# Attention mixed with a state-space branch on one core: a TensorE activity floor that runs to the last group, taps at their real weight, and the state-space output added by VectorE

## The chip, the cores and the metric

The kernel runs on one core of a Trainium2 chip. The metric is device time in microseconds (us) from one launch, lower is better. Three runs of the kernel before gave 757.92 to 760.72 us, median 759.01 us. A separate execution was recorded by the hardware profiler; it took 758.27 us, of which 756.5 us lie between its first and its last instruction (the span).

Engine names are those of the profile: PE (TensorE matmuls), PEld (its weight loads), DVE (VectorE), ACT (ScalarE), POOL (GpSimd), SP (SyncE, which here only issues DMAs).

## The reference, cut to what matters

```python
def _A_ref(x, wqkv, wo):                      # x: 1 x 2048 x 512, 32 heads of 16
    ...
    scores = jnp.einsum("bhqd,bhkd->bhqk", q, k) * scale
    p = _softmax(scores, axis=-1)
    o = jnp.einsum("bhqk,bhkd->bhqd", p, v)
    return (lambda x, *d: x.transpose(*d))(o, 0, 2, 1, 3).reshape(B, S, D) @ wo

def _B_ref(u, A_re, A_im, B_re, B_im, C_re, C_im, log_dt, Dskip):
    ...
    K = jnp.einsum("dn,dnl,dn->dl", Cc, P, dB).real       # a kernel of 2048 taps per channel
    ...                                                    # y: causal convolution of u with K, by FFT
    return y + u * Dskip[None, None, :]

g = _sigmoid((x * gate_w).sum(-1, keepdims=True))
return g * a + (1 - g) * b
```

## The kernel before

**Attention.** The scores of 32 heads are cut into 2048 tiles of 128 keys by 512 queries (`NSL`). Three tiles make a group; there are 683 groups (`NG`), counted by `g`. For each group PE multiplies keys and queries into one of two PSUM tiles (`SC0`, `SC1`; `qk`), ACT takes the exponential of the group into `ET` (or `EX`, the same ring's later slots; `ex`), and PE multiplies the result with the values into `OA` (`pv_mm`). An exponential of three tiles is 1536 columns wide ("3-wide"). In some groups the third tile is left to DVE and ACT does only two (1024 columns, "2-wide"): DVE writes scaled integers whose bits are a coarse exponential (`bits`, tile `DZ`), POOL makes three shifted copies of four such tiles (`batch`, tiles `DU`, `CUTS`), and PE multiplies all four versions with the values (`sums`). Four such tiles, from four groups, make a quad; the table `PACE` says how many quads should have begun by which group, and `WIN` how many buffers they have.

**State-space branch.** Projections and parameters come first. Then, 16 times, a block of the convolution kernel is computed by short matmuls of 48 or 64 columns, the taps, into the PSUM tile `MB` (`kstage`, `MB<-T,Z`), moved out by DVE (`Kt`, `Ks`) and written to DRAM (`gm_kd`). 32 times, the convolution itself reads it back as `H`, with the input as `U`, and multiplies the two (`ystage`, `MB<-U,H`); the results go to DRAM and come back as `Yl` and `Yl2`.

**Output.** For each of 16 blocks of 128 rows (`lt`) PE multiplies the normalized attention with `Wo` into `MB` and DVE moves the block into `fo`, which is stored (`outs`, `out_mm`). For the blocks 0 to 7 that DVE instruction also multiplies by the gate and adds `Yl`. For the blocks 8 to 15 PE adds `Yl` and `Yl2` with two matmuls by an identity (`out_y`, `idb`), and the eviction is a plain copy. Blocks 12 to 15 end after the last group, in code written out by hand (`part`, `side`, `ends`).

**The order.** Each engine's instructions are put in order when the kernel is built, by a planner (`Sched`, `Prog`) with costs written in the code; on the chip each engine runs its list in that order and waits on semaphores. For each group the planner places the exponential, the next group's `qk`, and then fills PE with other work until `OVER` us after the planned end of the exponential (`fill`). Besides, it keeps a count of TensorE activity in columns (the argument `a` of `mm`, summed in `p.act`): where a group has less than `want` (from `FILL`, `FILL2`), it adds matmuls of a zero tile `wm` (`zero`), four of 256 or 512 columns side by side into `OA`, `MB` or the next scores' bank, and one row strip beside the scores. Before, `want` is 0 from group `ZEND` on, and nothing is added there. `BG1`, `YGO` and `YLGO` name the events after which the second parameter quarter, the loads of `U` and `H`, and those of `Yl` may be issued on SP's queue; `BACK` is how far such a load may run ahead of the queue.

Of the kernel before, what the change touches and what calls it, by code (L numbers as in the profile page):

```python
# [11 lines left out]
ALU = mybir.AluOpType  # L12
# [3 lines left out]
D = 512  # L16
# [15 lines left out]
VLD = .0545  # L32
LAZY = 9
PDEL = 0.3
ZEND = 200
OUTP = 6
YSEG = 4
KSEG = 4
FILL = 1500
FILL2 = 1500  # L40
OVER = 0.4
REST = (14, 0, 1792, 425)
DLAG = .6
PLAG = .4
# [13 lines left out]
CUTS = (26, 56, 94)  # L58
XB = 128 * (127 - math.log2(5.3794))
WIN = ((0, 560, 2, 4), (560, 679, 4, 6))  # L60
PACE = ((0, 0), (40, 0), (90, 0), (140, 0), (200, 12.6), (270, 18.2), (340, 35.7), (420, 54.1), (500, 70.9), (570, 87.7), (630, 102.7), (683, 115.95))
DVEND = 679
YLP = 4.5
YQ = 0
XGO = 'g14'
YGO = 'g130'
YLGO = 'K14'
BG0 = 'g0'
BG1 = 'K1'
BG2 = 'K4'  # L70
BG3 = 'g0'
TP = 2
# [6 lines left out]
NZ = 2  # L79
US = [2, 12, 3]  # L80
HS = [4, 48, 8]
BACK = 0.3
UN4 = 4
HN = 1
UB = 1.10
# [643 lines left out]
def record(nc, p, B, ins):  # L729
# [709 lines left out]
    def kstage(blk):  # L1439
# [8 lines left out]
        for k in range(8):  # L1448
            for t in range(4):
                if t % KSEG == 0:  # L1450
                    yield ("PE", .062 * KSEG + (.06 if k + t == 0 else 0))
                lo, n = (0, 64) if t % 2 == 0 else (16, 48)
                at = (t // 2 * 112 + t % 2 * 64) * CB
                for j in range(4):
                    x = k ^ j
                    ch = 32 * (blk % 4) + 4 * (j // 2) + 2 * (j % 2) + 8 * (x % 4) + x // 4
                    mm(lambda j=j, x=x, lo=lo, n=n: MB(64 * x + lo, [[1, n]], 32 * j, 32), lambda ch=ch, t=t: Z(t // 2 * 4096 + ch, [[128, 32]]),
                       lambda ch=ch, at=at, n=n: Tm(at + 2 * (ch % 32), [[2 * CB, n // 2], [1, 2]]),
                       zk + [(Tm, (t, m), blk) for m in range(3 if t % 2 else 4)], ky, k + t == 0, t == 3, pos=(0, 32 * j),
                       c=.062 if j == 0 else 0, a=n // 2, cfg="C")  # L1460
# [202 lines left out]
    def outs():  # L1663
# [16 lines left out]
        for lt in range(13):  # L1680
            if lt == 12:
                yield ("AFTER", "n29")
            yield ("LOCK", "MB")
            for pi in range(4 if lt < 12 else 3):
                yield ("PE", MM)
                out_mm(lt, (MB, 0, 0), pi)
            for k in range(2 if lt >= 8 else 0):
                yield ("PE", MM)
                out_y(lt, (MB, 0, 0), k)
            if lt == 12:  # L1690
                break
            yield ("DVE", .7, -1)
            o, off, W = fo, (lt % 4) * D, [(fo, lt % 4, lt)]
            if lt < 8:
                op("DVE", lambda v, lt=lt, o=o, off=off: v.scalar_tensor_tensor(o(off, [[1, D]]), MB(0, [[1, D]]), B["g"](lt, [[1, 1]]),
                                                                                Yl(8 * lt, [[128, D // 8], [1, 8]]), ALU.mult, ALU.add),
                   [(MB, 0, ('o', lt))] + [(Yl, k) for k in range(NBLK)] + key("g"), W, c=.7)
            else:
                op("DVE", lambda v, o=o, off=off: v.tensor_copy(o(off, [[1, D]]), MB(0, [[1, D]])), [(MB, 0, ('o', lt))], W, c=.62)
# [145 lines left out]
    for g in range(NG):  # L1845
# [25 lines left out]
                    sch.force(f"dvp{i}")  # L1871
                sch.add(bits(g + 1), 0)
        t = p.tm["ACT"]
        want = (FILL if g < REST[3] else FILL2) * (t - t0) / 1.335 + min(max(lack, -256), 768)
        t0 = t
        sch.rest = g < REST[3] and g % REST[0] < REST[1]
        if sch.rest:
            want = max(want, REST[2])
        sch.fill(t, t + OVER, want if g < ZEND else 0)
        lack = want - p.act if g < ZEND else 0  # L1880
        p.act = bare = 0
        while lack >= 256 and p.tm["PE"] < t + OVER and g < NG - 1:
            z = zbank()
# [7 lines left out]
        p.act = 0  # L1891
    o = SC[(NG - 2) % 2]
    banks = [(MB, 0, 0), (o, 0, 0), (o, 512, 1), (o, 1024, 2)]
    part = [(lt, k) for lt in (13, 14) for k in range(5)]

    def piece(lt, k):
        if k < 3:
# [33 lines left out]
        side(0, h)  # L1931
    for i in range(3):
        out_mm(12 + i, banks[i], 3, True)
    for k in (1, 2, 3, 4, 5):
        for h in range(2):
            side(k, h)
    tail = [(fo, i * D, [(fo, i, 12 + i)]) for i in range(4)] + [(Qm, 0, [(Qm, (0, j), 'o') for j in range(4)])]
    ends = ((0, "DVE", 0, D), (1, "ACT", 0, D), (2, "DVE", 0, D), (3, "ACT", 0, w), (3, "DVE", w, w))
    for (i, eng, at, n), (f, o, W) in zip(ends, tail):
        b, off, sl = sides[1] if at else banks[i]  # L1940
        R = [(b, sl, ('o', 12 + i) if n == D else ('o', 15, at // w))]
        if eng == "DVE":
            op("DVE", lambda v, f=f, o=o, b=b, off=off, n=n: v.tensor_copy(f(o, [[1, n]]), b(off, [[1, n]])), R, W, c=.07 + n * .00108)
# [39 lines left out]
```

## Time and profile before

| | |
|---|---|
| median of 3 runs | 759.01 us (757.92 to 760.72) |
| profiled execution | 758.27 us |
| its span, first to last instruction | 756.5 us |
| mean granted TensorE clock | 0.986 of full speed |
| ACT busy | 737.4 us, 97% of the span |
| PE busy | 685.9 us, 91% |
| DVE busy | 656.2 us, 87% |
| POOL busy | 359.4 us, 48% |
| exponentials on ACT | 683, of them 453 2-wide and 230 3-wide |
| tiles left to DVE | 452, which is 113 quads |

The profile shows one execution. A group of instructions there has a line of the kernel, an engine, an operation and its tiles (`ET<-SC` is read "from `SC` into `ET`"), a count, the engine's busy time in it, and the idle time just before it with what ended that wait. A row of the timeline has a start, a length and the instructions merged in it.

### The profile page before, as it was taken

What the parts mean: (1) busy time and instruction counts of PE and PEld (TensorE: products, weight loads), DVE (VectorE), ACT (ScalarE), POOL (GpSimd) and SP (SyncE); (2) the same over time, 40 slices, a digit from 0 to 9 for tenths busy, and PEclk for the clock granted to TensorE, in tenths of its full rate; (3) what the DMA queues carried; (4) which work ended last, traced back from release to release, by engine and by line L of the source; (5) the groups of instructions that cost most, each with busy time, mean ns of one, the idle gap of its engine ahead of it and who ended that gap; (6) DMA issues with size and microseconds to landing.
All of it is one profiled execution on the core that took longest, in us unless ns stands there. A gap on an engine that the chain in (4) does not pass through costs nothing.

```text
span 756.5 us, 31064 instructions
## 1 busy us (share of the span) xinstructions
PE 685.9 (91%) x13740; PEld 288.5 (38%) x13741; DVE 656.2 (87%) x1096; ACT 737.4 (97%) x695; POOL 359.4 (48%) x356
## 2 busy tenths in 40 slices
PE   7777878887899987898999999999999999999998
PEld 3222333432445343355344444443453443222222
DVE  8999998689998898899898989898887878687886
ACT  7999999999999999999999999999999999999996
POOL 5000000000066631222777776767758777677683
PEclk9999999999999998999999999999999999999999
DMA  9657710421825777654478686613766784200001
GB/s 216 163 150 141 114 43 9 107 58 50 222 55 130 194 201 187 188 121 102 134 191 227 172 209 153 189 22 75 207 150 161 171 221 87 36 26 26 26 15 37
DMA packets 176587, 94.32 MB, mean 125 GB/s; under 512 B 116802, under 2 KB 159940, under 8 KB 176452
## 3 DMA queue, kind: packets, MB, share of 16 engines
q1 hardware_dynamic: 175636, 91.61, 49.5%
q8 instruction: 108, 1.77, 1.0%
q10 hardware_dynamic: 816, 0.72, 0.3%
q14 instruction: 27, 0.22, 0.1%
HBM read 63.42 MB, written 18.90 MB: 109 GB/s over the span
## 4 chain that ended last, share of the span: by engine, by line
ACT 76%; PE 18%; DVE 4%; POOL 1%; issue 1%; DVEq 0%; POOLq 0%
ACT ET L1007 68%; ACT EX L1007 8%; PE SC L744 7%; PE OA L744 7%; PE MB L744 3%; DVE DZ L1029 2%; POOL DU L1048 1%; DVE T L1093 1%; DVE OT L1069 0%; DVE ON L1084 0%; DVE ft L1093 0%; DVE Ks L1471 0%; DVE Qm L1819 0%; DVE OnT L1089 0%; DVE Kt L1468 0%
## 5 line engine op out<-in xcount | busy, mean ns | idle before, releaser
L1007 ACT ACTIVATE ET<-SC 128x1024 bf16<-128x1024 f32 (+1 forms) x618 | 675.0, 1341 | 8.2 <-PE SC L744 6.7
L1048 POOL INT64_ADD DU<-DZ x336 | 348.2, 1051 | 324.4 <-DVE T L1093 191.8
L1029 DVE TENSOR_SCALAR DZ<-SC 128x512 uint16<-128x512 f32 x452 | 302.3, 684 | 67.4 <-PE SC L744 55.0
L744 PE MATMUL SC<-Qm,KT 32*128 32x512 bf16 x2048 | 277.4, 389 | 60.1 <-ACT ET L1007 54.0
L744 PEld LDWEIGHTS SC<-Qm,KT 32*128 32x128 bf16 x2048 | 70.7, 91 | 265.5 <-ACT ET L1007 194.3
L744 PE MATMUL OA<-ET,VE 128*32 128x512 bf16 x1461 | 148.0, 393 | 1.2 <-DVE VE L853 0.9
L744 PE MATMUL OA<-DU,VE 128*32 128x512 bf16 x1356 | 130.1, 386 | 2.1 <-POOL DU L1048 2.0
L744 PEld LDWEIGHTS MB<-U,H 128*32 128x32 bf16 x4096 | 85.5, 144 | 29.4 <-issue 20.3
L744 PE MATMUL MB<-U,H 128*32 128x128 bf16 (+7 forms) x4096 | 94.6, 227 | 0.0
L1007 ACT ACTIVATE EX<-SC 128x1024 bf16<-128x1024 f32 (+1 forms) x65 | 69.0, 1273 | 0.0
L744 PEld LDWEIGHTS OA<-ET,VE 128*32 128x32 bf16 x1461 | 37.6, 96 | 59.7 <-issue 54.1
L1093 DVE TENSOR_TENSOR T<-B,DT 128x1536 bf16<-128x1536 bf16 x64 | 59.7, 966 | 0.0
L744 PEld LDWEIGHTS OA<-DU,VE 128*32 128x32 bf16 x1356 | 36.0, 98 | 41.2 <-issue 26.0
L744 PE MATMUL OA<-wm 128*32 128x256 bf16 (+3 forms) x242 | 47.6, 350 | 1.2 <-DVE idf L799 1.2
L744 PEld LDWEIGHTS MB<-T,Z 128*32 128x32 bf16 x2048 | 43.1, 156 | 11.6 <-issue 7.9
L744 PE MATMUL MB<-T,Z 128*32 128x48 bf16 (+1 forms) x2048 | 46.2, 236 | 0.1
L744 PE MATMUL OA<-DZ,VE 128*32 128x512 bf16 x452 | 45.0, 388 | 0.0
L1093 DVE TENSOR_TENSOR ft<-Z 128x512 f32<-128x512 f32 (+3 forms) x48 | 40.2, 862 | 0.1
L1093 DVE TENSOR_TENSOR Z<-ft,ft 128x1024 bf16<-128x1024 bf16 (+3 forms) x56 | 31.7, 566 | 0.4
L1621 POOL MEMSET gt<- 128x128 f32 x1 | 0.2, 206 | 58.1 <-DVE pt L1093 58.1
L1574 DVE TENSOR_TENSOR Yst<-MB,gt 128x512 bf16<-128x512 f32 x32 | 21.8, 681 | 6.7 <-PE MB L744 6.6
L1069 DVE STREAM_TRANSPOSE OT<-OA 128x512 f32<-128x512 f32 x32 | 22.6, 707 | 1.8 <-PE OA L744 1.6
(139 smaller groups left out, 428.9 us busy)
## 6 DMA issues: line engine op xcount, KB each, us to landing
H<-gm_kd SPq DMA_DIRECT2D x128, 256.0 KB, 4.0
U<-gm_xs SPq DMA_DIRECT2D x128, 134.2 KB, 3.4
T<-B SPq DMA_DIRECT2D x16, 256.0 KB, 3.6
gm_yd<-Yst SPq DMA_DIRECT2D x64, 64.0 KB, 3.1
gm_kd<-Ks SPq DMA_DIRECT2D x64, 40.0 KB, 2.2
gm_xs<-xP SPq DMA_DIRECT2D x16, 136.0 KB, 5.2
gm_pd<-L SPq DMA_DIRECT2D x8, 256.0 KB, 4.2
Z<-gm_pd SPq DMA_DIRECT2D x8, 256.0 KB, 3.5
```

The costliest lines, as they stand in the source:

```text
L744: op("PE", lambda t: t.matmul(out(), lhsT(), rhs(), start=start, stop=stop, skip_group_check=True, **kw), R, W, c=c, lat=.15, a=a, cfg=cfg)
L1007: op("ACT", lambda a: a.activation(E(at, [[1, 512 * n]]), sc(0, [[1, 512 * n]]), AF.Exp, scale=DH ** -0.5), [(sc, i, g) for i in range(n)] ...
L1029: op("DVE", lambda v: v.tensor_scalar(z.u16(512 * k, [[1, 512]]), sc(1024, [[1, 512]]), XS, XB, ALU.mult, ALU.add), [(sc, 2, g)], [(z, k, ...
L1048: op("POOL", lambda v, u=u, cut=cut: v.int64_add(u.u64(), z.u64(), cut * 0x0001000100010001), R, [(u, 0, i)], c=1.016, lat=.09, lk=True)
L1069: op("DVE", lambda v: v.transpose(OT(512 * w, [[1, 512]]), OA(0, [[1, 512]])), [(OA, 0, b)], [(OT, w, b)], c=.64)
L1093: op(eng, lambda v: v.tensor_tensor(o(), a(), b_(), f), R, W, c=c)
L1574: op("DVE", lambda v, w=w, h=h: v.tensor_tensor(Yst(1024 * w + 4 * h, [[128, R8], [8, 16], [1, 4]]), MB(0, [[1, R8], [R8, 16], [NC, 4]]), ...
L1621: op("POOL", lambda v: v.memset(B["gt"](0, [[1, NC]]), 0.0), [], [(B["gt"], j) for j in range(8)], c=.3)
```

## The change

The activity floor now goes on to the last group: up to group `ZEND` (200 before, 260 now) with 1500 columns for every 1.335 us of planned exponential, and after it with `LOW`, 1300; a group's surplus is carried over up to 256 columns in both stretches (`SURP`). The taps of `kstage` count a quarter of their columns as activity, where they counted half. PE may be filled to 0.5 us past the exponential, not 0.4. `PACE` asks for more quads early and in all (last entry 118.95, before 115.95). The events behind which loads are issued, and `BACK`, are changed. For output blocks 8 to 11, 12, 14 and the second half of 15, the matmul that adds `Yl` is left out and the DVE eviction adds it; blocks 13 and the first half of 15 keep it, since ACT evicts them. `Yl2` stays on PE.

```diff
-ZEND = 200
+ZEND = 260
...
+LOW = 1300
+SURP = 256
 FILL2 = 1500
-OVER = 0.4
+OVER = 0.5
...
-PACE = ((0, 0), (40, 0), (90, 0), (140, 0), (200, 12.6), (270, 18.2), (340, 35.7), (420, 54.1), (500, 70.9), (570, 87.7), (630, 102.7), (683, 115.95))
+PACE = ((0, 0), (40, 0), (90, 0), (140, 0), (200, 15.0), (270, 28.3), (340, 39.5), (420, 53.9), (500, 73.9), (570, 90.7), (630, 105.7), (683, 118.95))
...
-YGO = 'g130'
-YLGO = 'K14'
+YGO = 'projs'
+YLGO = 'K15'
 BG0 = 'g0'
-BG1 = 'K1'
+BG1 = 'g0'
...
-BACK = 0.3
+BACK = 0.4
...
-                       c=.062 if j == 0 else 0, a=n // 2, cfg="C")
+                       c=.062 if j == 0 else 0, a=n // 4, cfg="C")
...
-            for k in range(2 if lt >= 8 else 0):
+            if lt >= 8:
                 yield ("PE", MM)
-                out_y(lt, (MB, 0, 0), k)
+                out_y(lt, (MB, 0, 0), 1)
...
-                op("DVE", lambda v, o=o, off=off: v.tensor_copy(o(off, [[1, D]]), MB(0, [[1, D]])), [(MB, 0, ('o', lt))], W, c=.62)
+                op("DVE", lambda v, lt=lt, o=o, off=off: v.tensor_tensor(o(off, [[1, D]]), MB(0, [[1, D]]), Yl(8 * lt, [[128, D // 8], [1, 8]]), ALU.add),
+                   [(MB, 0, ('o', lt))] + [(Yl, k) for k in range(NBLK)], W, c=.68)
...
-        want = (FILL if g < REST[3] else FILL2) * (t - t0) / 1.335 + min(max(lack, -256), 768)
+        want = (FILL if g < ZEND else LOW) * (t - t0) / 1.335 + min(max(lack, -256 if g < ZEND else -SURP), 768)
...
-        sch.fill(t, t + OVER, want if g < ZEND else 0)
-        lack = want - p.act if g < ZEND else 0
+        sch.fill(t, t + OVER, want)
+        lack = want - p.act
...
-    part = [(lt, k) for lt in (13, 14) for k in range(5)]
+    part = [(13, k) for k in range(5)] + [(14, k) for k in (0, 1, 2, 4)]
...
-    for k in (1, 2, 3, 4, 5):
-        for h in range(2):
-            side(k, h)
+    for k, h in ((1, 0), (1, 1), (2, 0), (2, 1), (3, 0), (4, 0), (4, 1), (5, 0), (5, 1)):
+        side(k, h)
```

Since the planner decides, the whole order moves. Three places show it.

On ACT, each row is a run of exponentials of one width. Before, groups 206 to 243:

```order
L1007 ACTIVATE ET<-SC 128x1024 x4
L1007 ACTIVATE ET<-SC 128x1536 x8
L1007 ACTIVATE ET<-SC 128x1024 x4
L1007 ACTIVATE ET<-SC 128x1536 x12
L1007 ACTIVATE ET<-SC 128x1024 x4
L1007 ACTIVATE ET<-SC 128x1536 x6
```

Now, groups 190 to 241:

```order
L1009 ACTIVATE ET<-SC 128x1536 x2
L1009 ACTIVATE ET<-SC 128x1024 x20
L1009 ACTIVATE ET<-SC 128x1536
L1009 ACTIVATE ET<-SC 128x1024 x20
L1009 ACTIVATE ET<-SC 128x1536
L1009 ACTIVATE ET<-SC 128x1024 x8
```

Groups 200 to 259 had 24 2-wide exponentials and have 52; groups 280 to 399 had 113 and have 81; over the whole kernel 453 became 461 and 230 3-wide ones became 222. The quads rise from 113 to 115.

On PE, groups 577 to 582, behind the last convolution step and ahead of the first output block (`OA` sums values, `DU`, `DZ`, `ET` and `EX` are the exponentials' tiles). Before:

```order
L744 MATMUL OA<-DU_68,VE 32x512 x4
L744 MATMUL OA<-ET,VE 32x512 x4
L744 MATMUL SC<-Qm,KT 128x512 x6
L744 MATMUL OA<-EX,VE 32x512 x4
L744 MATMUL SC<-Qm,KT 128x512 x6
L744 MATMUL OA<-DZ_65,VE 32x512 x4
L744 MATMUL OA<-EX,VE 32x512 x2
L744 MATMUL OA<-ET,VE 32x512 x2
L744 MATMUL SC<-Qm,KT 128x512 x3
L744 MATMUL OA<-DU_69,VE 32x512 x4
```

Groups 575 to 577 now:

```order
L746 MATMUL OA<-DZ_64,VE 32x512 x4
L746 MATMUL MB<-Wo,OnR_73 32x512 x4
L746 MATMUL OA<-DU_66,VE 32x512 x4
L746 MATMUL SC<-Qm,KT 128x512 x3
L746 MATMUL OA<-EX,VE 32x512 x4
L746 MATMUL OA<-DU_67,VE 32x512 x4
L746 MATMUL MB<-Wo,OnR_73 32x512 x8
L746 MATMUL SC<-Qm,KT 128x512 x3
```

The output blocks (`MB<-Wo,OnR`) began in groups 580 to 599 and now begin in groups 560 to 579, so that this stretch has them between the scores.

At the end of PE's list, the last output blocks. Before:

```order
L744 MATMUL SC<-Wo,OnT_72 128x512 x2
L744 MATMUL SC<-Wo,OnT_72 128x256 x4
L744 MATMUL SC<-Yl,idb 128x256 x2
L744 MATMUL SC<-Yl_103,idb 128x256 x2
L744 MATMUL SC<-Wo,OnT_72 128x256 x2
```

Now:

```order
L746 MATMUL SC<-Wo,OnT_72 128x512 x2
L746 MATMUL SC<-Wo,OnT_72 128x256 x4
L746 MATMUL SC<-Yl,idb 128x256
L746 MATMUL SC<-Yl_103,idb 128x256 x2
L746 MATMUL SC<-Wo,OnT_72 128x256 x2
```

One half-width matmul fewer stands ahead of the last one. The zero matmuls go from 259 to 374: by groups, from 127 to 126 in 0 to 79, from 103 to 136 in 80 to 139, from 29 to 100 in 140 to 259, and from 0 to 12 from there on. On SP's queue the four loads of the second parameter quarter (`Z_154`) move from behind the first block written to `gm_kd` to ahead of it, and the first load of `U` comes 15 rows of that queue later.

More of the change, by code (lines that the diff above doesn't have):

```diff
@@ L1942, in record @@
         if eng == "DVE":
-            op("DVE", lambda v, f=f, o=o, b=b, off=off, n=n: v.tensor_copy(f(o, [[1, n]]), b(off, [[1, n]])), R, W, c=.07 + n * .00108)
+            op("DVE", lambda v, f=f, o=o, b=b, off=off, n=n, at=at, i=i: v.tensor_tensor(f(o, [[1, n]]), b(off, [[1, n]]), Yl(8 * (12 + i) + 16 * at, [[128, n // 8], [1, 8]]), ALU.add),
+               R + [(Yl, x) for x in range(NBLK)], W, c=.07 + n * .0012)
         else:
```

## Prediction

> **What bounds the kernel now.** First the page: how long each engine works, and the groups of ACT and DVE.
>
> ```profile
> span 756.5 us, 31064 instructions
> PE 685.9 (91%) x13740; PEld 288.5 (38%) x13741; DVE 656.2 (87%) x1096; ACT 737.4 (97%) x695; POOL 359.4 (48%) x356
> L1007 ACT ACTIVATE ET<-SC 128x1024 bf16<-128x1024 f32 (+1 forms) x618 | 675.0, 1341 | 8.2 <-PE SC L744 6.7
> L1029 DVE TENSOR_SCALAR DZ<-SC 128x512 uint16<-128x512 f32 x452 | 302.3, 684 | 67.4 <-PE SC L744 55.0
> ```
>
> ACT is busy for 97% of the span, and nearly all of it is the exponentials, with only 8.2 us of idle time before them, 6.7 of it ended by PE's scores. So the time falls in only two ways: ACT gets less to do, or it waits less. An engine beside it counts only where it makes ACT wait. The chain of waits gives the price of an exponential, since it shows runs without a gap:
>
> ```profile
> 13.63 57.76 ACT ET L1007 x43
> 646.09 2.75 ACT EX L1007 x3
> ```
>
> The first run is 3-wide: 57.76 / 43 = 1.343 us each. The second is 2-wide: 2.75 / 3 = 0.917. A tile given to DVE takes 0.426 us from ACT.
>
> Next, where ACT waits. The timeline of ACT shows these idle times (in brackets) in three neighbourhoods:
>
> ```profile
> 283.50 1.02 ACT L1007 ACTIVATE ET<-SC 128x1024 bf16<-128x1024 f32 x1 [0.21 <-PE SC L744]
> 285.00 18.06 ACT L1007 ACTIVATE ET<-SC 128x1024 bf16<-128x1024 f32 x14 [0.47 <-PE SC L744]
> 303.53 1.02 ACT L1007 ACTIVATE ET<-SC 128x1024 bf16<-128x1024 f32 x1 [0.47 <-PE SC L744]
> 304.89 40.95 ACT L1007 ACTIVATE ET<-SC 128x1024 bf16<-128x1024 f32 x34 [0.34 <-PE SC L744]
> 346.10 58.02 ACT L1007 ACTIVATE ET<-SC 128x1024 bf16<-128x1024 f32 x59 [0.25 <-PE SC L744]
> 651.80 2.12 ACT L1007 ACTIVATE ET<-SC 128x1024 bf16<-128x1024 f32 x2 [0.21 <-PE SC L744]
> ```
>
> One exponential alone lasts 1.02 us, but in a run only 0.917 pass from one to the next. So whenever ACT stops, 0.10 us is lost besides the idle time shown. What is special about these moments is in the windows, whose column after POOL is the granted TensorE clock:
>
> ```profile
> 277.90:281.30 3.40, 1.83 (x50) 0.83 (x46) 3.40 (x6) 3.40 (x3) 0.00 (x0) 1.00 0.54 135
> 281.40:284.80 3.40, 3.40 (x56) 1.28 (x52) 2.70 (x5) 2.92 (x3) 0.00 (x0) 0.50 0.88 247
> 295.00:298.40 3.40, 2.10 (x69) 1.14 (x59) 2.76 (x6) 3.40 (x4) 0.00 (x0) 1.00 0.81 245
> 298.50:305.30 6.80, 6.21 (x127) 2.88 (x124) 5.69 (x10) 5.99 (x6) 0.00 (x0) 0.50 0.77 215
> 339.40:342.80 3.40, 1.66 (x37) 0.67 (x25) 3.40 (x7) 3.40 (x4) 0.00 (x0) 1.00 0.52 129
> 342.80:346.20 3.40, 3.40 (x95) 1.80 (x98) 2.44 (x6) 3.15 (x4) 0.00 (x0) 0.50 0.90 259
> 646.60:650.00 3.40, 2.16 (x24) 0.52 (x22) 3.21 (x6) 3.40 (x5) 0.73 (x1) 1.00 0.39 82
> 650.00:653.40 3.40, 3.40 (x29) 0.61 (x26) 1.91 (x4) 3.12 (x4) 2.33 (x3) 0.50 0.02 5
> 73.20:76.60 3.40, 3.40 (x31) 0.73 (x29) 2.26 (x4) 3.24 (x3) 0.00 (x0) 0.50 0.29 52
> 140.00:160.00 20.00, 16.96 (x484) 9.52 (x475) 14.17 (x34) 20.00 (x16) 0.00 (x0) 1.00 0.39 104
> ```
>
> In the first eight rows the clock falls to half four times, for 3.4 or 6.8 us, and ACT is short of work in or right behind it. Ahead of each fall PE (first number after the length) was busy for 1.66 to 2.16 of 3.40 us, 49 to 64%. From 140 to 160 us, where the kernel adds zero matmuls, it is busy for 85% and the clock stays full.
>
> The Trainium skill ("TensorE: Matmul & The Clock Gate", Part 1 on the HAM clock gate) says the clock goes to half after about one idle window of 3.4 us, and that gaps over about 3 us are to be avoided. By that rule a PE half busy would keep its clock, and a floor of activity would buy nothing. The lengths of 3.4 and 6.8 us agree with the window; the falls at 49 to 64% busy do not agree with a need for idleness, and I go by the rows.
>
> ACT's remaining waits lie mostly in one stretch of dense 2-wide groups with taps and convolution (its row from 400 to 560 us):
>
> ```profile
> L1007 ACT ACTIVATE ET<-SC 128x1024 bf16<-128x1024 f32 (+1 forms) x157 | 151.5, 1092 | 4.5 <-PE SC L744 3.4
> ```
>
> **The change part by part.**
>
> *Quads.* 230 3-wide exponentials become 222, so 8 x 0.426 = **3.4 us** less on ACT. It costs DVE 8 x 0.684 = 5.5 us and, with three shifted versions of each tile, PE 24 more value matmuls, six quartets. A quartet takes PE 0.22 us, the step between these starts:
>
> ```profile
> 287.76 0.40 PE L744 MATMUL OA<-DU,VE 128*32 128x512 bf16 x4
> 287.99 0.39 PE L744 MATMUL OA<-ET,VE 128*32 128x512 bf16 x4
> 130.92 0.38 PE L744 MATMUL SC<-Qm,KT 32*128 32x512 bf16 x1 [0.41 <-ACT ET L1007]
> 130.92 0.39 PE L744 MATMUL OA<-wm 32*128 32x512 bf16 x1
> ```
>
> That is 1.3 us on PE. DVE has 5.8 us free from 140 to 160 alone, and the second parameter quarter, whose loads now come earlier on SP's queue, can fill that. If the cover is gone, a late DVE holds the scores' bank and ACT waits for up to those 5.5 us.
>
> *Zero matmuls.* Of the 115 added, 23 are row strips beside the scores, which start with them (130.92 both) and cost nothing. The other 92 are 23 quartets, 15 of 256 columns at half of 0.22 (an estimate from the full one) and 8 of 512: 15 x 0.11 + 8 x 0.22 = 3.4 us of PE, most of it in groups 80 to 259, where PE had 15% free at 140 to 160. I take 0 on the path; uncovered it is 3.4.
>
> *The clock.* The falls at 281, 298 and 343 us stand in groups 216 to 270, from which the floor was missing and which were 3-wide. Now those groups are nearly all 2-wide with three shifted versions each. Counting the order by the 0.22 quartet, groups 220 to 239 had 18 value quartets in 6 x 0.917 + 14 x 1.343 = 24.3 us and have 31 in 18.8 us; per us, 0.74 became 1.65, and 56 of 80 short convolution steps remain. The fall at 650 stands between the last convolution step and the first output block (groups 577 to 582, shown with the change); output quartets now stand there. So I expect these four gone. The rows give 0.21 + 0.47 + 0.47 + 0.34 + 0.25 + 0.21 = 1.95 us of idle time, and six stops at 0.10: **2.6 us**. Bounds: 0 if the clock falls elsewhere instead, and 2.6 if it doesn't. PE's order up to group 79 changes in one place only, so the fall at 73 us (the row ahead of the last) stays.
>
> *Fill to 0.5 us.* PE's work beside the scores may start the next scores 0.1 us later. The waits of PE's weight loads say how often that can matter:
>
> ```profile
> PEld SC L744 <- ACT ET L1007: 197.3, 397, 1.4
> PEld SC L744 <- ACT EX L1007: 22.7, 48, 0.8
> ```
>
> In 445 of 683 groups PE stood waiting for ACT, and 0.1 us is hidden. In the other 238 it might not be: 0 to 23.8 us. ACT's 6.7 us of waits for scores came in 20 pieces; so I stay near zero and take 0, keeping the other end as a rival.
>
> *Dense groups moved early.* Groups 200 to 259 get 28 more 2-wide exponentials, groups 280 to 399 have 32 fewer. The stretch from 400 to 560 lost 4.5 us in 160, 0.5 per 18 us; three more such stretches early cost 1.5, and six lighter ones later return up to that. I take 0, bounds +2.5 and -4.5 (all of those waits gone).
>
> *Evictions.* Five quartets of `Yl` leave `MB`: 1.1 us of PE, mostly in the last 100 us, off the path.
>
> ```profile
> L1574 DVE TENSOR_TENSOR Yst<-MB,gt 128x512 bf16<-128x512 f32 x32 | 21.8, 681 | 6.7 <-PE MB L744 6.6
> L1695 DVE SCALAR_TENSOR_TENSOR fo<-MB,g,Yl 128x512 bf16<-128x512 f32 x8 | 5.9, 743 | 0.3 <-PE MB L744 0.3
> L1699 DVE CAST fo<-MB 128x512 bf16<-128x512 f32 x4 | 2.7, 680 | 0.0
> ```
>
> The add of PSUM and `Yl` is not in the trace; it lies between 0.680 (copy) and 0.743 (multiply and add `Yl`). The two-operand instruction nearest to it takes 0.681. At the very end, PE:
>
> ```profile
> 752.35 0.60 PE L744 MATMUL SC<-Yl,idb 128*128 128x256 bf16 x4
> 752.78 0.38 PE L744 MATMUL SC<-Wo,OnT 128*128 128x256 bf16 x2
> 753.20 0.42 DVE L1943 CAST Qm<-SC 128x256 bf16<-128x256 f32 x1 [0.17 <-PE SC L744]
> 753.81 0.45 SPq L1947 DMA_DIRECT2D out_dram<-Qm x1
> ```
>
> Four `Yl` matmuls take 0.43 us, one goes: **0.1 us** from the last chain, 0 if the adding eviction is slower by 0.06. The full-width one that goes from block 14 stood under the last DVE transposes and brings nothing.
>
> *Loads.* `U` and `H` are asked for later by 15 rows of SP's queue, behind the parameters. No wait of PE for a load of `U` or `H` is among the longest waits of the trace. I take 0; one `H` load that is issued late costs at most its way of 4.0 us:
>
> ```profile
> H<-gm_kd SPq DMA_DIRECT2D x128, 256.0 KB, 4.0
> ```
>
> **Sum**: 3.4 + 2.6 + 0.1 = 6.1 us. The profiled execution took 758.27, so it would take 752.2; it lay 0.7 below the median of the three runs, 759.01, and against that the forecast is **752.9 us**.
>
> **The rivals.**
>
> 1. *The floor doesn't do what it says*: the clock falls as often, in other groups (280 to 340, now lighter). Only quads and tail remain: 759.0 - 3.5 = 755.5. For it: the floor is counted by the planner's clock, not the chip's, and places only 12 of its zeros past group 259. Against: those groups have more value work than the ones that fell. The skill's rule above gives the same 755.5, since the falls would not be PE's half-idleness.
> 2. *Waits come back in the dense early groups*, 2.5 us: 755.4. Together with 1: 758.0. For it: ACT waits there already in the row from 400 to 560.
> 3. *Waits shrink*, since groups 280 to 399 are lighter: up to 4.5 less, 748.4.
> 4. *Slower*: the fill to 0.5 us. The place is the scores of the 238 groups in which PE was not waiting. If half of them pass on the full 0.1 us, it is +11.9: 759.0 - 6.1 + 11.9 = 764.8. It makes the kernel slower by over 0.5% from 99 groups on (6.1 + 3.8 = 9.9 us). Against: ACT stopped for scores only 20 times.
>
> **How the numbers follow.** Forecast (750.5 to 755.2): 0.52. Rival 1: 0.14. Rival 2: 0.10. Both: 0.07. Rival 3: 0.10. Rival 4: 0.07. The range from 748.5 to 757.5 holds all but rivals 4, both, and some of 3: about 0.8. A measurement of this kernel can tell about 0.5% from no change, which is 755.2 to 762.8. Below it are the forecast, rival 3 and somewhat less than half of rivals 1 and 2, which stand at its edge: 0.72. Within it: the rest of these and both together, 0.21. Above: 0.07.
>
> **What would show it.** Right: no row of half clock between 200 and 740 us; 461 2-wide exponentials; ACT's idle time before exponentials at about 6 us instead of 8.2; three `Yl` matmuls of 256 columns at the end. Wrong: rows of half clock in new places (rival 1); new stops of ACT at full clock between 220 and 290 us (rival 2) or many of about 0.1 us everywhere, with fewer waits of PE's weight loads for ACT than 445 (rival 4).

## The result and the profile after

The changed kernel takes **754.44 us** (753.50 to 756.03, 6 runs); the kernel before, measured beside it, took 758.46 (757.62 to 760.72, 6 runs). The ratio is 0.9944, with a 95% interval of 0.9924 to 0.9963: 4.2 us less, within 2.8 to 5.8. The profiled execution took 754.11 (span 752.3); that of before took 758.27 (756.5).

The page of the changed kernel, with its engines and the groups of ACT and DVE:

```profile
span 752.3 us, 31289 instructions
PE 686.2 (91%) x13857; PEld 288.5 (38%) x13858; DVE 659.4 (88%) x1104; ACT 732.2 (97%) x695; POOL 365.1 (49%) x362
L1009 ACT ACTIVATE ET<-SC 128x1024 bf16<-128x1024 f32 (+1 forms) x619 | 671.6, 1336 | 8.9 <-PE SC L746 5.1
L1031 DVE TENSOR_SCALAR DZ<-SC 128x512 uint16<-128x512 f32 x460 | 307.8, 684 | 64.8 <-PE SC L746 53.2
```

There are eight DVE tiles more (460 against 452, which is 115 quads against 113; where an expectation below writes 114 and 106 quads, it means these two numbers), and ACT is busy for 5.2 us less. But its idle time ahead of the exponentials has not fallen from 8.2 to 6, as the prediction wanted; it is 8.9.

The clock, by windows (the column after POOL is the granted TensorE clock), first for before and then for the change:

```profile
200.00:740.00 540.00, 512.62 (x10338) 217.99 (x10330) 465.83 (x754) 532.48 (x535) 343.58 (x332) 0.98 0.52 132
```

```profile
200.00:740.00 540.00, 516.30 (x10367) 217.44 (x10363) 463.81 (x751) 532.69 (x541) 353.40 (x342) 1.00 0.54 133
```

The falls between 200 and 740 us are gone. Yet ACT is busy for as long in these 540 us (532.69 against 532.48): nothing was won there in waits. The timeline of ACT shows what came in their place:

```profile
217.74 1.94 ACT L1009 ACTIVATE ET<-SC 128x1024 bf16<-128x1024 f32 x2 [0.36 <-PE OA L746]
220.03 19.80 ACT L1009 ACTIVATE ET<-SC 128x1024 bf16<-128x1024 f32 x21 [0.35 <-PE SC L746]
240.28 3.77 ACT L1009 ACTIVATE ET<-SC 128x1024 bf16<-128x1024 f32 x4 [0.45 <-PE SC L746]
244.68 14.94 ACT L1009 ACTIVATE ET<-SC 128x1024 bf16<-128x1024 f32 x15 [0.64 <-PE SC L746]
260.11 21.14 ACT L1009 ACTIVATE ET<-SC 128x1024 bf16<-128x1024 f32 x22 [0.49 <-PE OA L746]
287.94 12.45 ACT L1009 ACTIVATE ET<-SC 128x1024 bf16<-128x1024 f32 x13 [0.64 <-PE SC L746]
432.77 1.02 ACT L1009 ACTIVATE ET<-SC 128x1024 bf16<-128x1024 f32 x1 [0.83 <-PE SC L746]
434.38 4.69 ACT L1009 ACTIVATE ET<-SC 128x1024 bf16<-128x1024 f32 x5 [0.58 <-PE SC L746]
```

All of these stops are at full clock, and six of the eight stand in the dense early groups, at 217 to 288 us.

To add them up, each exponential is held against its pitch (0.917 us 2-wide, 1.343 3-wide): what it ends later behind its predecessor is ACT's waiting. In us, by stretches of groups:

| groups | before | after |
|---|---|---|
| 0–139 | 0.97 | 2.29 |
| 140–259 | 3.35 (2.29 of it at falls) | 4.79 |
| 260–399 | 3.57 (0.37 at a fall) | 3.73 |
| 400–499 | 4.10 | 1.87 |
| 500–682 | 1.55 (0.76 at a fall) | 0.15 |
| all | 13.5 | 12.8 |

The span fell by 4.2 us: 3.4 by the quads, 0.7 by waits. The falls took 3.4 us with them, but waits at full clock and a window of half clock at 14.7 us gave most of it back.

What ends the stop at 244.68 is seen on four engines. Beside ACT's row above, the rows are those of DVE, POOL and PE from the changed kernel's timeline:

```profile
241.51 1.22 DVE L1095 TENSOR_TENSOR ft<-Z 128x1024 f32<-128x1024 f32 x1
242.83 3.07 POOL L1050 INT64_ADD DU<-DZ  x3 [1.46 <-DVE ft L1095]
243.92 0.40 PE L746 MATMUL OA<-DU,VE 128*32 128x512 bf16 x4 [0.59 <-POOL DU L1050]
244.25 0.40 PE L746 MATMUL SC<-Qm,KT 32*128 32x512 bf16 x4
```

POOL waits 1.46 us until DVE's two-operand instruction is done, so its shifted version comes late; PE waits 0.59 us for that version, and the next scores stand behind it in PE's order. ACT then waits 0.64 us for the scores. The stop at 287.94 has the same form; of the other four early stops none has a wait of PE for `DU` ahead of it.

At 432 us it is a load. SP's queue and PE:

```profile
426.55 0.52 SPq L1532 DMA_DIRECT2D U<-gm_xs  x1
427.12 2.52 SPq L1544 DMA_DIRECT2D H<-gm_kd  x4
431.23 1.18 PE L746 MATMUL MB<-U,H 128*32 128x128 bf16 x48 [0.77 <-DMA H<-gm_kd]
433.57 0.45 PE L746 MATMUL MB<-U,H 128*32 128x128 bf16 x16 [0.47 <-DMA H<-gm_kd]
```

SP issues without a pause, so the four `H` loads go out from 427.12 on, and PE gets to their matmuls before the last ones land. ACT loses 2.2 us in groups 363 to 369.

The end of the program:

```profile
748.01 0.49 PE L746 MATMUL SC<-Yl,idb 128*128 128x256 bf16 x3
748.13 1.31 SPq L1950 DMA_DIRECT2D out_dram<-fo  x3
748.76 0.42 DVE L1945 TENSOR_TENSOR Qm<-SC,Yl 128x256 bf16<-128x256 f32 x1
749.49 0.45 SPq L1950 DMA_DIRECT2D out_dram<-Qm  x1
```

There are three `Yl` matmuls of 256 columns, as predicted, and the last eviction ends at 749.18. But SP is busy with three other stores until 749.44, and the last store begins right behind them, so the tenth of a microsecond is not won.

### The profile page after: what moved, and what is told of

Its sections match the earlier page's. It is cut to its first block, busy times and chain, and to the rows that moved or that the text cites. A ratio compares the mean times of both kernels' runs of the same rounds, so it can differ in the third digit from the quotient of the medians.

```text
span 752.3 us, 31289 instructions
## 1 busy us (share of the span) xinstructions
PE 686.2 (91%) x13857; PEld 288.5 (38%) x13858; DVE 659.4 (88%) x1104; ACT 732.2 (97%) x695; POOL 365.1 (49%) x362
## 3 DMA queue, kind: packets, MB, share of 16 engines
q8 instruction: 109, 1.79, 1.0%
## 4 chain that ended last, share of the span: by engine, by line
ACT 77%; PE 17%; DVE 3%; DMA 1%; POOL 1%; issue 0%; SPq 0%; DVEq 0%; ACTq 0%; POOLq 0%
ACT ET L1009 70%; PE SC L746 7%; ACT EX L1009 7%; PE OA L746 7%; PE MB L746 4%; DMA H<-gm_kd 1%; DVE DZ L1031 1%; POOL DU L1050 1%; DVE ft L1095 0%; DVE Qm L862 0%; DVE T L1095 0%; DVE Qm L1822 0%; DVE OT L1071 0%; DVE OnT L1091 0%; DVE KT L846 0%
## 5 line engine op out<-in xcount | busy, mean ns | idle before, releaser
L1050 POOL INT64_ADD DU<-DZ x342 | 353.9, 1049 | 372.7 <-DVE DZ L1031 257.3
L1031 DVE TENSOR_SCALAR DZ<-SC 128x512 uint16<-128x512 f32 x460 | 307.8, 684 | 64.8 <-PE SC L746 53.2
L746 PE MATMUL SC<-Qm,KT 32*128 32x512 bf16 x2048 | 274.6, 385 | 50.9 <-ACT ET L1009 44.9
L746 PE MATMUL OA<-DU,VE 128*32 128x512 bf16 x1380 | 132.4, 385 | 2.5 <-POOL DU L1050 2.4
L746 PEld LDWEIGHTS MB<-U,H 128*32 128x32 bf16 x4096 | 83.5, 144 | 30.7 <-issue 20.5
L746 PE MATMUL MB<-U,H 128*32 128x128 bf16 (+7 forms) x4096 | 92.6, 226 | 2.1 <-DMA H<-gm_kd 1.5
L746 PE MATMUL OA<-wm 128*32 128x256 bf16 (+3 forms) x317 | 59.9, 343 | 1.2 <-DVE idf L801 1.2
L746 PE MATMUL MB<-T,Z 128*32 128x64 bf16 (+1 forms) x2048 | 46.6, 235 | 0.0
L1095 DVE TENSOR_TENSOR ft<-Z,DM 128x1024 bf16<-128x1024 bf16 x32 | 21.4, 680 | 0.0
```

The lines of the kernel that those rows point to most:

```text
L746: op("PE", lambda t: t.matmul(out(), lhsT(), rhs(), start=start, stop=stop, skip_group_check=True, **kw), R, W, c=c, lat=.15, a=a, cfg=cfg)
L1031: op("DVE", lambda v: v.tensor_scalar(z.u16(512 * k, [[1, 512]]), sc(1024, [[1, 512]]), XS, XB, ALU.mult, ALU.add), [(sc, 2, g)], [(z, k, ...
L1050: op("POOL", lambda v, u=u, cut=cut: v.int64_add(u.u64(), z.u64(), cut * 0x0001000100010001), R, [(u, 0, i)], c=1.016, lat=.09, lk=True)
L1095: op(eng, lambda v: v.tensor_tensor(o(), a(), b_(), f), R, W, c=c)
```

## The experiments

The two theories at the start: **A**, the time comes from the quads and from the falls that are gone, and the floor's zeros hold the clock; **B**, the new stops in dense groups (by zeros, quads or their packing) eat what the falls gave. Every run here was compared with the kernel before on its own chip; ratios are to that.

**The order without its zeros.** Zero matmuls from group 140 on are planned, but not emitted.

```
        zero(...)
+       if p.q >= 140: p.drop.add(len(p.log) - 1)
```

> The changed kernel's order, with the 111 zero matmuls that it adds from group 140 on left out of the program and nothing else moved. Theory A (the added zeros hold the clock): half-clock windows return between 200 and 450 us, three or more, and the time is 1 to 3 us above the changed kernel, about 756 us. Rival B (the quads' value matmuls, moved early, hold the clock, and the zeros only stand in the way): no half-clock window between 200 and 740 us, and the stops of ACT between 215 and 290 us, which lose 4.8 us there now, shrink; the time is 1 to 3 us below the changed kernel, 751.5 to 753.5 us.

756.63 us, ratio 0.9967 (0.9949 to 0.9985). That is above the change by 2.2 us in the medians and by 1.7 in the ratios, whose intervals overlap a little. The stops stay, though two of them are shorter (at groups 156 and 198, 0.30 and 0.32 us lost instead of 0.46 and 0.60). ACT's timeline of this kernel:

```profile
264.27 3.82 ACT L1012 ACTIVATE ET<-SC 128x1024 bf16<-128x1024 f32 x4 [0.50 <-PE SC L747]
268.52 20.41 ACT L1012 ACTIVATE ET<-SC 128x1024 bf16<-128x1024 f32 x21 [0.42 <-PE SC L747]
289.56 2.85 ACT L1012 ACTIVATE ET<-SC 128x1024 bf16<-128x1024 f32 x3 [0.64 <-PE SC L747]
```

The first of these rows stands right behind a fall of the clock at 261 us, the only one of this profile between 200 and 740 us, where theory A wanted three or more. By the mean granted clocks of the runs, 3.7 windows of half clock (3.41 us each) passed per run; of the changed kernel, 1.8; of before, 6.5. So the zeros do hold the clock, and for the most part they are not what makes the dense stops. But of the 4.6 windows that the change saves, 2.8 are saved without these zeros, by the denser order and the zeros ahead of group 140.

**The old pace of quads in the changed kernel** (113 quads, floor and all else kept): `PACE` as before.

> The changed kernel with the old table of quads (453 2-wide exponentials, 113 quads, few of them in groups 200 to 279), the floor, the taps' weight, the 0.5 us and the evictions kept; the planner then adds 419 zeros. Theory A (quads are worth 3.4 us, and what the dense early groups lose in waits comes from elsewhere): 3.4 us above the changed kernel, 757.9 us. Rival B (the dense early groups give 3.4 us and take about as much in new waits): within 1 us of the changed kernel, 753.5 to 755.5 us, with no half-clock window after 100 us and fewer stops between 200 and 290 us.

759.66 us, ratio 1.0005 (0.9989 to 1.0021), 5.2 above the change and 1.8 above theory A's time, although only 2.2 windows of half clock passed per run. With the floor and without the two added quads, the change is worth nothing.

**The floor in the old kernel, at the falls only**: zeros are allowed in groups 212–220, 229–241, 263–270 and 574–583, and the rest is planned anew behind them.

```
+LOWS = ((212, 221), (229, 242), (263, 271), (574, 584))
+        on = g < ZEND or any(a <= g < b for a, b in LOWS)
-        lack = want - p.act if g < ZEND else 0
+        lack = want - p.act if on else 0
```

> The kernel before with zeros allowed in four short runs of groups (212 to 220, 229 to 241, 263 to 270, 574 to 583), 52 zero matmuls more, the same 453 2-wide exponentials in the same groups. Theory A (a fall of the clock costs about 0.8 us in stops of ACT, four of them 3.4 us): the four falls go and the time is 3 to 3.4 us below the kernel before, 755.1 to 755.5 us. Rival B (zeros and a new order bring waits of the same size): the falls go, and the time stays within 1 us of the kernel before.

758.72 us, ratio 0.9994 (0.9981 to 1.0007). No half clock from 18 to 755 us in the profile, 2.5 windows per run, and no gain, as rival B had it. The planner placed later work otherwise, and new waits of 1.7 us came in groups 300 to 319.

**The fill to 0.5 us in the old kernel**: `OVER = 0.5`.

> The kernel before with PE filled to 0.5 us past the exponential, not 0.4, alone. Theory A (scores that start up to 0.4 us late cost nothing, and few are later): within 1 us of the kernel before, 757.5 to 759.5 us. Rival B (late scores pass the 0.1 us on to ACT): 2 us or more above the kernel before, 760.5 us or more, with more than 20 stops of ACT for the scores.

763.00 us, ratio 1.0048 (1.0030 to 1.0067). The time is rival B's, but not its cause: ACT's waits are 14.2 us, against 13.5 before, and PE ended 18 of its stops ahead of exponentials, where rival B wanted more than 20. The loss is at the end, in PE's rows:

```profile
750.29 0.43 PE L744 MATMUL MB<-Yl,idb 128*32 128x512 bf16 x4
751.67 1.05 PE L744 MATMUL MB<-Wo,OnR 128*32 128x512 bf16 x16 [0.95 <-DVE fo L1699]
752.53 0.66 PE L744 MATMUL MB<-Yl,idb 128*32 128x512 bf16 x8
754.06 0.83 PE L744 MATMUL MB<-Wo,OnT 128*32 128x512 bf16 x12 [0.86 <-DVE fo L1699]
```

Output blocks that had stood between scores were pushed past the last exponential, where one waits for the other's eviction. ACT's wait for its first eviction grew from 3.69 to 8.41 us.

**Zeros put into the old order.** Nothing is planned anew: a quartet of 512-column zeros behind the fill of the same groups where a sum in `OA` is open (32 quartets).

```
+        for k, q, b in reversed(prog.inj):
+            log[k:k] = [(prog.op, q, a) for a in zeros(wm, bufs["OA"], b)]
```

> The kernel before, order word for word as it was, with 32 quartets of 512-column zero matmuls put in behind the fill of groups 212-220, 229-241, 263-270 and 574-583 (nothing else moved, nothing left out). They add to the open sum in OA. Theory A (the falls at 281, 298, 343 and 650 us cost what the profile's pitch shows, 3.4 us, and zeros beside ACT cost nothing): no half clock between 200 and 700 us in the profile, median 758.7 - 3.4 = 755.3, ratio 0.9955 (about 0.994 to 0.997). Rival B (a fall only uncovers a wait that comes anyway, a few groups later; this is why the replanned order with zeros gained nothing): the falls go and the time stays, 758 to 759, ratio 0.999 or more. Rival C (the zeros themselves make scores late): new stops of ACT at the inserted places, time up by up to 32 x 0.22 = 7 us.

758.44 us, ratio 0.9990 (0.9972 to 1.0008). By the mean clocks 2.4 windows of half clock passed per run instead of 6.5, and the time hardly moved. But two of the falls stayed in the profile, at 283 and 297 us, where too few sums were open, so this run alone does not settle the price of a fall. It showed another wait, on PE inside a run of equal matmuls:

```profile
426.02 0.82 PE L757 MATMUL OA<-DU,VE 128*32 128x512 bf16 x10 [0.56 <-issue]
```

**`BACK` at 0.3 in the changed kernel**; the order is the same up to group 340.

> The changed kernel with BACK back at 0.3: the order is the same up to about group 340, and the state-space loads and matmuls from there to group 500 are planned earlier or later by some groups. Theory A (the stop of PE at 431-434 us for an H load, 2.2 us of ACT, comes from the loads being issued late by the new BACK and SP's queue): that stop goes, ACT's excess in groups 340 to 479 falls from about 5.5 to 3.5, median about 752.3, ratio to before 0.992. Rival B (the wait moves to another H load or to other groups): 754.4 within 0.8, ratio 0.994.

753.34 us, ratio 0.9929 (0.9906 to 0.9953), the lowest of all, though its interval overlaps the change's. The stop at 432 us is gone (2.17 us in groups 360 to 379 became 0.39), so it was the place of that load. But the waits came back behind it: groups 380 to 399 waited 1.79 us instead of 0.75, and groups 400 to 499 2.74 instead of 1.87, so that groups 360 to 499 waited 4.9 in all, against 4.8. This is rival B for the waits. The first of the new ones is ended by this stop of PE:

```profile
450.92 0.76 PE L746 MATMUL MB<-U,H 128*32 128x128 bf16 x36
452.67 0.62 PE L746 MATMUL MB<-U,H 128*32 128x120 bf16 x28 [0.99 <-issue]
```

**All quads and the floor, but a later pace.**

```
-PACE = (..., (200, 15.0), (270, 28.3), (340, 39.5), (420, 53.9), ...
+PACE = (..., (200, 12.6), (270, 20.2), (340, 37.1), (420, 54.1), ...
```

> The changed kernel with all its 114 quads and its floor, but a pace near the old one for groups 160 to 420 (12.6, 20.2, 37.1, 54.1 quads at 200, 270, 340, 420): groups 200 to 279 have 39 2-wide exponentials instead of 67, groups 280 to 399 have 112 instead of 81. Theory A (the 3.6 us of new waits in groups 140 to 259 come from the dense early packing): ACT's excess in groups 140 to 259 falls from 4.8 to about 1.5, groups 280 to 399 gain back less than 1.5; the clock stays full by the floor; median 754.4 - 2 = 752.4, ratio 0.992. Rival B (stops go with 2-wide groups wherever they stand): what is saved early is lost in 280 to 399, 754.4 within 0.8. Rival C (the floor does not hold in 3-wide groups, which fell before): half clock at 260 to 345 us again, 756 to 758.

755.62 us, ratio 0.9958 (0.9943 to 0.9972). Groups 140 to 259 waited 2.8 instead of 4.8 us, and 260 to 399 waited 5.7 instead of 3.7: of the three, rival B is nearest, and 2.0 us of stops went with the 2-wide groups. The rest did not. In ACT's rows of this kernel, the first two stops of the change stand where they stood, and a long one is new:

```profile
217.73 1.94 ACT L1009 ACTIVATE ET<-SC 128x1024 bf16<-128x1024 f32 x2 [0.37 <-PE OA L746]
220.02 42.52 ACT L1009 ACTIVATE ET<-SC 128x1024 bf16<-128x1024 f32 x43 [0.35 <-PE SC L746]
263.47 3.84 ACT L1009 ACTIVATE ET<-SC 128x1024 bf16<-128x1024 f32 x4 [0.93 <-PE SC L746]
267.88 33.08 ACT L1009 ACTIVATE ET<-SC 128x1024 bf16<-128x1024 f32 x28 [0.57 <-PE SC L746]
```

Held against the old pace (ratio 1.0005), the same kernel with two quads, eight tiles, fewer, it prices the quads in their place: 0.0047 of 759 is 3.6 us, with about 1.6 either way by the two intervals, near the 3.4 that was worked out. The order moved between the two as well, so the nearness is in part luck.

**The evictions undone in the changed kernel**, for blocks 8 to 12 (block 12 then holds its `Yl` part twice).

```
+            for k in range(2 if lt >= 8 else 0): ... out_y(lt, (MB, 0, 0), k)
-                op("DVE", ... v.tensor_tensor(..., MB(0, [[1, D]]), Yl(...), ALU.add) ...)
+                op("DVE", ... v.tensor_copy(..., MB(0, [[1, D]])) ...)
```

> The changed kernel with the eviction edits of output blocks 1 to 11 undone (both Yl quartets in MB for blocks 8 to 11, plain copies for 1 to 7 as before for their second half; the tail edits stay). Theory A (those quartets lie beside ACT's work and cost nothing): 754.4 within 0.6, ratio 0.9945. Rival B (as with the fill of 0.5 alone, four more quartets push the last output blocks behind the last exponential): later part and tail longer by 1 us or more, 755.4 or above, ratio 0.996 or more, and the last group of exponentials to the end of the span longer than 10.6 us.

755.43 us, ratio 0.9945 (0.9924 to 0.9966): no difference, since the kernel before took 759.15 on that chip. Five dense stops of the change came back at the same groups with the same lengths (0.47, 0.45, 0.56, 0.74 and 0.75 us lost at groups 156, 158, 179, 183 and 226): they belong to the order, not to chance.

**Zeros beside the values, old order kept**: 32 quartets in groups 213 to 271 and 12 in 573 to 581, each right behind a value quartet.

> The kernel before with its order kept and zero quartets of 512 columns put right behind value quartets: 32 in groups 213-271 (256 PE instructions, as many as one 16 KB fetch of them, so that the fetches stand where they stood from group 272 on) and 12 in groups 573-581. Nothing is left out. The earlier insertion left two of the falls (windows at 0.316 and 0.337 of full-array columns) and moved PE's fetches by 192 instructions from group 271 to 574. Theory A (the falls cost 3.4 to 4 us and zeros beside values cost little): no half clock from 200 to 740 us, no new stop of PE inside a run of equal matmuls, median about 755.5, ratio 0.9955 or less. Rival B (what the falls give back is lost again, as in the two kernels with zeros before): ratio 0.998 or more although the falls are gone.

758.24 us, ratio 1.0000 (0.9984 to 1.0016). The clock is full; one stretch by windows, of before and then of this kernel:

```profile
277.90:305.30 27.40, 21.80 (x492) 10.29 (x488) 23.75 (x38) 25.91 (x22) 3.67 (x3) 0.81 0.71 190
```

```profile
277.90:305.30 27.40, 24.16 (x618) 11.70 (x610) 24.30 (x40) 27.28 (x23) 4.48 (x4) 1.00 0.77 205
```

ACT is busy for 27.28 us of it, against 25.91, and groups 140 to 259 wait 2.16 instead of 3.35 us. So the falls there do cost time, but of the 2.3 us that the pitch puts down to them, 1.2 came back. The zeros, or the waits that the falls had hidden, cost something too; at the fourth place:

```profile
647.28 2.11 ACT L1030 ACTIVATE EX<-SC 128x1024 bf16<-128x1024 f32 x2 [0.92 <-PE SC L767]
```

Groups 560 to 579 wait 1.42 us that they did not wait before, twice what the fall at 650 had cost. In all, ACT waits 0.9 us less than before where 3.4 us of falls went, and the ratio shows none of it: rival B.

**The quads alone in the old kernel** (only `PACE`, as in the later pace, so 115 quads).

> The kernel before with 114 quads instead of 106 and nothing else (pace 12.6, 20.2, 37.1, 54.1 at 200, 270, 340, 420, then that of the changed kernel; 461 2-wide exponentials). Theory A (a quad is worth 0.426 us of ACT, DVE and PE cover it): median 759.1 - 3.4 = 755.7, ratio 0.9955, with falls of the clock as before. Rival B (DVE at 87% cannot cover them, new waits for scores behind DVE's reads of the bank): 757.5 or more, ratio 0.998 or more, DVE's TENSOR_SCALAR ending ACT's new stops.

762.89 us, ratio 1.0054 (1.0032 to 1.0075), slower. The time is rival B's, but not its cause: PE waited 0.9 us for DVE's reads of the scores' bank, as before. ACT's waits are 22.8 us. Some are falls in dense groups; others are POOL again, with DVE's `T` ahead of it:

```profile
508.40:511.80 3.40, 3.40 (x41) 0.91 (x36) 3.19 (x7) 2.79 (x3) 2.15 (x3) 0.50 0.02 5
505.40 3.10 POOL L1048 INT64_ADD DU<-DZ  x3 [1.03 <-DVE T L1093]
506.49 0.40 PE L744 MATMUL OA<-DU,VE 128*32 128x512 bf16 x4 [0.99 <-POOL DU L1048]
```

In all, PE waited 4.9 us for `DU` in front of its value matmuls, against 2.0 before and 2.4 in the change.

**The load order alone in the old kernel**: `YGO`, `YLGO` and `BG1` as changed.

> The kernel before with the parameters' second quarter asked for from the start and the Yl and state-space gates as in the change, nothing else (453 2-wide, old fill, old zeros): convolution matmuls come some groups earlier and the output blocks begin at group 560 instead of 580. Theory A (load order costs nothing by itself): 759.1 within 0.8, ratio 0.999 to 1.001. Rival B (the reordered middle costs what the floor gains, H loads are late at 295 to 310 and 430 us as in the runs on the changed kernel): 761 or more, ratio 1.003 or more, with PE waiting for H for over 1 us in all. Rival C (an earlier end of the convolution lightens the last 100 us): ratio below 0.998.

764.32 us, ratio 1.0069 (1.0043 to 1.0096). Slower as rival B said, but not by its cause: PE had no long wait for `H`. The waits are 9.6 us in groups 260 to 399, 3.3 of them at 354 to 365 us, where the clock stood at half for three windows.

**Floor, quads and loads together**, with the fill, `BACK`, the evictions and the end as before.

> The kernel before with three parts of the change together: the floor with its new count of taps, 114 quads (at the pace of the run with the quads alone) and the load order; fill to 0.4 us, BACK 0.3, evictions and tail stay as before. Alone, the quads measured 1.0054, the loads 1.0069 and, without replanning, the floor's zeros 1.000. Theory A (parts don't add: the quads and the loads lost because the clock fell in 8 to 9 windows of 3.4 us, in dense groups too, and the floor takes that away): 754.5 to 756.5, ratio 0.994 to 0.997, at most one half-clock window from 200 to 700 us, ACT's waits below 15 us. Rival B (parts add): 759.1 + 4.1 + 5.2 - at most 1 = 767, ratio about 1.01. Rival C (as A, but the last output blocks end late, as with the fill of 0.5 alone, since 17 of their quartets stand in the last three groups instead of 5): ACT's waits as in A, but the stretch from the last exponential to the end longer than 10.7 us by 2 to 5 us, 757 to 761.

765.45 us, ratio 1.0075 (1.0047 to 1.0103). Theory A is out: past 100 us the clock fell once only, and ACT still waited 22.6 us. The largest stop:

```profile
331.76 2.05 POOL L1050 INT64_ADD DU<-DZ  x2 [4.07 <-DVE T L1095]
332.85 0.40 PE L746 MATMUL OA<-DU,VE 128*32 128x512 bf16 x4 [1.00 <-POOL DU L1050]
335.69 1.02 ACT L1009 ACTIVATE ET<-SC 128x1024 bf16<-128x1024 f32 x1 [3.83 <-PE OA L746]
```

POOL sat idle for 4.07 us, most of it behind four `T` instructions in a row on DVE (3.57 us), and ACT lost 3.8. The end is 2.1 us longer as well (5.83 instead of 3.69 us to ACT's first eviction), as rival C had it. B's 767 is near, but by waits that neither part alone had.

ACT's waits in us by groups, in one profiled execution each, with the half-clock windows of 3.41 us per run (mean of all runs):

| kernel | 0–139 | 140–259 | 260–399 | 400–499 | 500–682 | all | windows | ratio |
|---|---|---|---|---|---|---|---|---|
| before | 1.0 | 3.4 | 3.6 | 4.1 | 1.5 | 13.5 | 6.5 | 1 |
| change | 2.3 | 4.8 | 3.7 | 1.9 | 0.1 | 12.8 | 1.8 | 0.9944 |
| `BACK` 0.3 | 1.3 | 4.5 | 2.6 | 2.7 | 0 | 11.0 | 1.8 | 0.9929 |
| later pace | 2.4 | 2.8 | 5.7 | 2.5 | 1.0 | 14.3 | 1.7 | 0.9958 |
| old pace | 1.3 | 4.6 | 4.1 | 3.4 | 3.8 | 17.2 | 2.2 | 1.0005 |
| without zeros | 3.1 | 5.4 | 2.8 | 1.8 | 1.0 | 14.0 | 3.7 | 0.9967 |
| evictions undone | 1.6 | 4.4 | 2.4 | 2.0 | 1.1 | 11.5 | 1.6 | 0.9945 |
| old, floor at falls | 2.3 | 1.1 | 4.3 | 4.4 | 0.7 | 12.7 | 2.5 | 0.9994 |
| old, fill to 0.5 | 2.2 | 5.3 | 2.8 | 2.8 | 1.1 | 14.2 | 5.4 | 1.0048 |
| old, zeros put in | 1.2 | 4.3 | 4.3 | 4.0 | 1.7 | 15.4 | 2.4 | 0.9990 |
| zeros beside values | 1.2 | 2.2 | 3.0 | 4.0 | 2.3 | 12.6 | 1.7 | 1.0000 |
| quads alone | 1.2 | 2.6 | 6.6 | 8.0 | 4.5 | 22.8 | 5.7 | 1.0054 |
| loads alone | 1.3 | 2.1 | 9.6 | 4.7 | 1.4 | 19.0 | 6.1 | 1.0069 |
| three parts | 3.5 | 1.4 | 10.4 | 6.2 | 1.2 | 22.6 | 2.3 | 1.0075 |

One profile's sum is not exact: the change and the kernel with its evictions undone share their stops and still differ by 1.3 us, and the profiled executions of the old pace, of the zeros put in, and of the quads alone took 3.3, 2.6 and 2.0 us more than the medians of their runs.

## Why the prediction was right, and where it was not

The time, 754.4, lies 1.5 us above the 752.9 forecast and inside its range, and 1.0 below the 755.4 of rival 2. The two large terms went the way that was forecast, and one that was put at nothing did not. That the sum is so near is partly luck, since errors of both signs cancel: apart from the four falls, waits grew by 3.7 us in groups 140 to 259, by 0.5 in 260 to 399 and by 1.3 ahead of them, and shrank by 2.2 in groups 400 to 499 and by 0.6 behind.

- **Quads, 3.4 us: right**, 3.41 in the span's account, which closes with it and 0.7 of waits, and 3.6 between the later and the old pace, within wide bounds. But it holds only in a fitting order: alone, the same eight tiles made the old kernel 4 us slower. The prediction's cover, "DVE has 5.8 us free", looked at DVE's time and not at POOL, which waits behind DVE's long instructions.
- **The clock, 2.6 us: the falls went as forecast, and their price was set too low.** The four falls went, by the zeros and by denser groups both, and had cost 3.4 us by the pitch: the prediction added only the stops it listed, not the late exponentials after them (0.18 and 0.10 us at groups 237 and 239, for one). Over 192 runs of 14 kernels, each held against its own kernel's mean, a half-clock window more went with 0.78 us more (correlation 0.80). At 6.5 against 1.8 windows that is 3.6 us. No run shows this gain by itself: in the old kernel, zeros in three ways brought the windows from 6.5 to 2.5, 2.4 and 1.7, and the ratios were 0.9994, 0.9990 and 1.0000. There the zeros, or the order that came with them, took what the falls gave.
- **Dense groups moved early, 0 us: the step that failed.** Apart from the falls, groups 140 to 259 waited 1.1 us and now wait 4.8, so 3.7 us where 1.5 was reckoned from the row of 400 to 560 us. The lighter groups paid nothing back in sum: groups 260 to 399, which have 24 2-wide exponentials fewer, waited 3.2 us apart from the fall there and now wait 3.7, with 2.2 of it at a late load. What fell, by 2.2 us, is the waiting of groups 400 to 499, and they are not lighter: 90 of them are 2-wide in both kernels, and they hold 672 convolution matmuls now, against 592. Why they wait less is open. This is rival 2, with its sign in the profile as foretold (new stops at full clock between 220 and 290 us). It did not replace the gain of the clock, it ate about as much. That these stops belong to the 2-wide groups is shown in part: with the later pace 2.0 of the 3.7 us moved with those groups, but 1.7 stayed, with 76 2-wide groups from 140 to 259 against 72 before and 104 in the change. That remainder comes with some other part of the new order. POOL behind DVE was read from the rows of two of the six early stops, and no run took it away.
- **Loads, 0 us: one load came late**, 2.2 us at 432 us, about half of the 4.0 that had been put as the most. With `BACK` at 0.3 it was on time, and other waits of the same sum came behind it, so what it costs the whole is open.
- **Fill to 0.5 us, 0 us: right for the scores.** PE's weight loads waited for ACT in 456 groups, not in fewer than 445:

```profile
PEld SC L746 <- ACT ET L1009: 201.8, 407, 1.4
PEld SC L746 <- ACT EX L1009: 21.4, 49, 0.8
```

Rival 4 is out in its mechanism; but alone the fill cost 0.48% by pushing output blocks past the last exponential, which no rival had. The output blocks of the change begin about 20 groups earlier, and its last stretch waits 0.1 us only.

- **Evictions, 0 us: right** (0.9945 without them). **The end, 0.1 us: nothing**, since SP's stores set it. **Zeros, 0 us**: in the changed order they pay, if anything; left out from group 140 on, the time rises by 1.7 us by the ratios, which their intervals hardly tell from nothing.
- **Early half clock**: 1.3 us more than in the profile of before, from a window at 14.7 us. A window that starts between 12 and 15 us is in 11 of the 14 profiles, of either order, and absent from that of before, so it looks like chance and no part of the change.

What stays open: the parts do not add. Alone, quads, loads and fill measured +0.5, +0.7 and +0.5%, zeros 0.0; three of them together +0.75%, and all edits -0.56%. Each new order came with waits of 11 to 23 us, and the runs name them only after the fact, most of them without a cause.

## What to carry over

Where numbers steer a planner, work out separately what the edit does (ACT's work, the clock) and what the new order costs in waits: the first came out to within 1 us here, the second varied by 12 us between orders. Before a tile is moved to an engine with free time, look at who waits behind that engine's longest instructions, here POOL and, through PE's order, the scores. And test a part inside the whole as well as alone: the two added quads were worth about 3.6 us in one order and cost 4 in another.

## What the runs showed of the hardware

- **The falls are not fixed.** 79 runs of the kernel before had a mean granted clock of 0.978 to 1.000. The ten at 0.990 or more averaged 756.9 us, the seventeen at 0.982 or less 760.8.
- **No sharp threshold.** Counted from the trace of before, with a quartet of 512 columns taken to fill the array for its 0.22 us, the windows of 3.41 us ahead of the four late falls were filled to 24 to 33%, and the one ahead of the fall at 73 us to 43%; two windows of 35 and 36%, at 326 and 305 us, passed without a fall. In the kernel with zeros put in, a window of 33% at 314 us passed, and a fall followed one of 35% at 293. (Some matmul records can be missing from a trace, so the shares are rough.) The rule of the Trainium skill ("TensorE: Matmul & The Clock Gate", Part 1 on the HAM clock gate) that the clock falls after an idle window does not fit: PE was busy for 49 to 64% of those four windows, and zeros added there (0.81 to 1.00 in the two rows of the zeros beside values) kept the clock up.
- **PE seems to stop for its own instructions.** The row of the queue that brings them (packets, MB, share), in the changed kernel's page of the profile:

```profile
q8 instruction: 109, 1.79, 1.0%
```

For 27,715 matmuls and weight loads that is 254 for each packet of 16 KB. The idle 0.99 us at 452.67 us above, inside a run of equal matmuls with no wait, follows a packet that was fetched from 450.1 to 451.3 us. The 14 profiles have 19 such stops of over 0.25 us, up to 1.35, and each of them ends 1.25 to 1.62 us after a packet landed, while packets are about 7 us apart. So it looks as if PE, where matmuls are short and dense, comes to the end of its instructions before the next packet can be used. No run tested that by itself.
